# Fourier mixing and RWKV channel mix: half of batch 1's first x load moved ahead of the receptance weights

## The chip, the cores and the metric

The kernel runs on one core of a Trainium2 chip. The metric is device time in microseconds (us); lower is better. A profiled execution lists every instruction of the engines: TensorE (PE in the profile, its weight loads PEld), VectorE (DVE), ScalarE (ACT), GpSimd (POOL) and SyncE (SP), and the traffic of the 16 DMA engines.

## The reference

The input x has 8 batches of 3072 rows and 256 columns, in fp32. First comes a Fourier mixing, then an RWKV channel mix on its result:

```python
X = np.fft.fft(np.fft.fft(x, axis=1), axis=2).real
x_prev = X shifted by one row, first row zero
xk = mu_k * X + (1 - mu_k) * x_prev
xr = mu_r * X + (1 - mu_r) * x_prev
k = np.maximum(xk @ w_k, 0)                 # 256 -> 1024
out = sigmoid(xr @ w_r) * ((k * k) @ w_v)   # w_r 256 -> 256, w_v 1024 -> 256
```

## The kernel before, in words

**The work per batch.** The sequence of 3072 rows is cut into 96 groups of 32 rows (batch 0), or into two sets of 48 (batches 1 to 7; one set on partitions 0 to 47, the other on partitions 64 to 111). Each batch is loaded in two halves, h = 0 and 1. A half consists of a direct part, `xp` (9 or 8 rows of 256 for each partition, `load_p`, L129), and of a mirrored part, `xm` (`load_m`, L144, an indirect gather of 8 rows for each partition, and for h = 0 one more row, `load_m0`). Both are cast from fp32 to fp16 on the way. `fold` (L161) adds `xp` to `xm` read backwards into `p`, on VectorE; its two instructions are L173 and L175. `butterfly` (L206) or `quarters_1` and `quarters_2` split `p` further. Then follow the sequence transform in two matmul stages with a twist between them (`a_...`, `d_...`, `c_...`; evacuated from PSUM by L572 on VectorE or L574 on ScalarE), the token shift with mu (`diff` L856, `scaled` L868, `mixed` L879), and the channel mix in chunks of 512 rows: `k_products` (L914), relu (L924), square (L934 on VectorE or L932 on ScalarE), the receptance in `r_item` (L941, sigmoid L946), the value in `v_tile` (L955) or, for the first chunks, in four parts in `v_part` (L967), and the final product `v_out` (L977 on VectorE, then an output DMA from SyncE).

**Buffers.** `xp` and `xm` have three buffers each, taken in turn by half batch (`x_tiles`, L120). Half (1, 0) uses xp buffer 1, half (1, 1) buffer 2, half (2, 0) buffer 0, half (2, 1) buffer 1, half (3, 0) buffer 2. PSUM gives three tiles psW of two banks and two tiles psV of one bank.

**The padding rows.** A few matmuls read partitions 0 to 111 of the folded data as a whole, with zero weights on partitions 48 to 63. What lies there must be a number. In batches 1 to 3 `load_p` therefore reads 64 partitions for the first set rather than 48. From batch 4 on it reads 48, and what is left in the buffers from before serves as padding.

**The order of the work.** The order is written out by hand. A loop over steps (L1245) emits for each step a piece of a chunk's key product and then what is listed for this step: `at(step, f, ...)` and `event(step, ...)`, L1107 to L1239. `pin_order` (L89) then keeps each engine in the order in which the instructions were emitted. An engine that waits holds everything behind it.

**The queue of loads.** All casting loads and gathers are issued by POOL, in order. `load_gate` (L495) lets VectorE write a single element that POOL then overwrites (L497), so that POOL cannot run ahead of VectorE past this point. At the time in question POOL issues: `loads` (L479: the key weights `wk` for forward chunks, the value weights `wv_sb`, some index tables), then `loads_0` (a gate, then the two receptance gathers `wr_sb[0]`), at step 1 `loads_1` (a gate, then half (1, 0): the two sets of `xp`, the single mirrored row, the large mirrored gather), at step 4 `loads_2` (two key gathers, half (1, 1), two receptance gathers, the identity table of `quarter_rows`), and at steps 9, 12 and 13 the halves (2, 0), (2, 1) and (3, 0). The receptance weights are read first by `r_item` at step 5. The fold of half (1, 0) stands at step 8, that of half (1, 1) at step 11, that of half (2, 0) at step 16.

Of the kernel before, what the change touches and what calls it, by code (L numbers as in the profile page):

```python
# [39 lines left out]
def kernel(  # L40
# [10 lines left out]
    nc = tc.nc  # L51
# [4 lines left out]
    N1, R = 48, 64  # L56
# [52 lines left out]
    xp_sb = [const.tile([112, 9, 256], FP16, name=f"xp{n}") for n in range(3)]  # L109
# [10 lines left out]
    def x_tiles(b, h):  # L120
        xp_t[b, h] = xp_sb[(2 * b + h - 1) % 3] if b or h else xp_00
        xm_t[b, h] = xm_sb[(2 * b + h) % 3]
# [3 lines left out]
    def parts(b):  # L126
        return 112 if b else 96

    def load_p(b, h, q0=0):  # L129
        r, n = 9 * h + q0, 9 - h - q0  # L130
        if b:
            for g in range(2):
                k = 64 if g == 0 and b < 4 else N1
                src = dataclasses.replace(x[b, 32 * g + r:32 * g + r + 1, :],
                                          ap=[[64 * D, k], [D, n], [1, D]])
                nc.gpsimd.dma_start(out=xp_t[b, h][64 * g:64 * g + k, 0:n], in_=src)  # L136
            return
        src = dataclasses.replace(x[b, r:r + 1, :], ap=[[32 * D, 96], [D, n], [1, D]])
        nc.gpsimd.dma_start(out=xp_t[b, h][0:96, q0:q0 + n], in_=src)

    def gather(dst, src, idx):
        nc.gpsimd.indirect_dma_start(dst, None, src, bass.IndirectOffsetOnAxis(ap=idx, axis=0))  # L142

    def load_m(b, h, o, n, idx):  # L144
        gather(xm_t[b, h][0:parts(b), XM0 + o:XM0 + o + 256 * n],
               x.rearrange("b (s r) d -> (b s) (r d)", r=n), idx)

    def load_m0(b):
        if b == 0:
            gather(xm_00[:, 1:257], x.rearrange("b s d -> (b s) d"), idx_0[:, 0:1])  # L150
        else:
            load_m(b, 0, 2048, 1, idx_g0[:, b:b + 1])

    def load_xh(b, h):
        x_tiles(b, h)
        load_p(b, h)
        if h == 0:
            load_m0(b)
        load_m(b, h, 0, 8, idx_g8[:, b, h:h + 1])
# [102 lines left out]
    for h in range(2):  # L262
        x_tiles(0, h)
    load_p(0, 0, 5)
    for xm in xm_sb:
        V.memset(_v(xm, XM0 + 2048, [(256, 2)]), 0.0)
# [22 lines left out]
    iota(idx_4, pattern=[[-1, 2]], base=S // 4 - 3, channel_multiplier=-8)  # L289
    load_m(0, 0, 0, 8, idx_8[:, 0, 0:1])  # L290
    load_p(0, 1)
    load_m(0, 1, 1024, 4, idx_4[:, 0:1])
    load_m(0, 1, 0, 4, idx_4[:, 1:2])
# [163 lines left out]
    turn = const.tile([P, P], FP16)  # L457
    mu_n = const.tile([P, 2, 2], FP32)

    def mirrored_mu():  # L460

        for a in range(2):
            V.tensor_copy(out=mu_m[:, a], in_=mu_f[:, 1 - a])
        V.tensor_copy(out=mu_m[0:1], in_=mu_f[0:1])
# [30 lines left out]
    def load_gate():  # L495
        V.memset(gate, 0)  # L496
        iota(gate, pattern=[[0, 1]], base=0, channel_multiplier=0)  # L497

    def loads_0():
        load_gate()  # L500
        for a in range(2):
            gather(wr_sb[0][a], moe_w_r, row_i[:, a:a + 1])

    def loads_1():
        load_gate()
        load_xh(1, 0)

    def loads_2():
        for a in range(2):
            gather(wk_sb[1][a], moe_w_k, row_i[:, 2 + a:3 + a])  # L510
        load_xh(1, 1)
        for a in range(2):
            gather(wr_sb[1][a], moe_w_r, row_i[:, 2 + a:3 + a])
        quarter_rows()

    def eo_sine():
# [27 lines left out]
    def quarter_rows():  # L544
        iota(same_i, pattern=[[0, 2], [1, 64]], base=0, channel_multiplier=-1)
        nc.gpsimd.tensor_scalar(out=same, in0=same_i, scalar1=0.0, scalar2=None,
                                op0=ALU.is_equal)
# [562 lines left out]
    diff(0, 4, 8)  # L1110
    mix_part(0, 0, 4, 8)
    loads_0()
    d_small(0, 10, 2)
    diff(0, 8, 16)
# [4 lines left out]
    event(3, (half_tables,))  # L1119
    event(4, (c_item, 0, 17, 8))  # L1120
    at(1, loads_1)
    at(4, loads_2)
    at(8, fold, 1, 0)
    at(5, r_item, (0, 0, 0))
    at(5, c_item, 0, 25, 2)
    at(5, diff, 0, 16, 24)
    at(5, mirrored_mu)
    at(6, mix_part, 0, 0, 16, 24)
    at(9, butterfly, 1, 0, 1)
# [3 lines left out]
    at(9, r_item, (0, 0, 1))  # L1133
    at(9, mix, 0, 0, 1, 1)
    at(9, load_xh, 2, 0)
    at(10, mix_part, 0, 1, 16, 24)
    event(11, (a_sums, 1, 0, 0), (a_sums, 1, 0, 4))
# [164 lines left out]
```

## Time and profile before

| what | value |
|---|---|
| median of 3 runs | 427.22 us (426.31 to 427.66) |
| profiled execution | 426.86 us |
| its span, from the first to the last instruction | 425.1 us |
| granted TensorE clock | 0.998 |
| VectorE busy | 371.7 us (87%) |
| ScalarE busy | 332.4 us (78%) |
| GpSimd busy | 63.2 us (15%) |

How to read it: a row of the timeline has the start of the instruction or of a group of equal ones, the busy time, the engine, the line of the code, the operation, what is written and read, and the number of instructions. Brackets at its end give the engine's idle time just before it and what ended that. Matmuls are pipelined, and their ends are modelled, so two groups can overlap in the list; the starts are what to compare. In the answer by stretches each engine has its busy time and in parentheses its instructions; then come the granted clock, the mean busy share of the 16 DMA engines (it can go a little over 1, since packets overlap) and GB/s.

### The profile page before, as it was taken

The numbers are of one execution on the slowest core, as the hardware profiler recorded it, in microseconds if no ns is written. First come the engines' busy times: TensorE is split into PE (matmuls) and PEld (weight loads), VectorE is DVE, ScalarE is ACT, GpSimd is POOL, SyncE is SP. The second block draws the span as 40 slices with busy tenths as digits, with TensorE's granted clock in tenths as the row PEclk, the third lists the DMA queues.
The fourth block names the chain that finished last, engine by engine and source line by source line (L and its number), as shares of the span: only waits on it lengthen the run. The fifth ranks groups of instructions, "written<-read, shape, count | busy, mean of one in ns | idle before, by whom it ended". The sixth has DMA issues, their size and how long they took to land.

```text
span 425.1 us, 9716 instructions
## 1 busy us (share of the span) xinstructions
PE 417.9 (98%) x4008; PEld 292.8 (69%) x4008; DVE 371.7 (87%) x593; ACT 332.4 (78%) x438; POOL 63.2 (15%) x99
## 2 busy tenths in 40 slices
PE   8999999999999999999999999999999999999996
PEld 3766766776767767676767776777777776776765
DVE  8998999999898999989999899989999676977553
ACT  7889887698769986699767996689876897666661
POOL 7478400200060001400032000500000000000000
PEclk9999999999999999999999999999999999999999
DMA  8879972632376222942349232772233232332333
GB/s 171 111 115 212 229 162 56 123 92 69 74 141 157 57 70 56 210 107 51 71 75 227 51 76 55 136 173 59 52 74 76 53 75 51 74 74 53 74 76 99
DMA packets 35280, 42.64 MB, mean 100 GB/s; under 512 B 4146, under 2 KB 31140, under 8 KB 35236
## 3 DMA queue, kind: packets, MB, share of 16 engines
q1 hardware_dynamic: 27488, 25.41, 24.0%
q0 software_dynamic: 7440, 16.36, 22.2%
q8 instruction: 31, 0.51, 0.5%
q10 hardware_dynamic: 308, 0.26, 0.2%
q14 instruction: 13, 0.11, 0.1%
HBM read 33.20 MB, written 25.17 MB: 137 GB/s over the span
## 4 chain that ended last, share of the span: by engine, by line
PE 90%; DVE 6%; DMA 2%; issue 1%; POOL 1%; ACT 0%; DVEq 0%; POOLq 0%
PE psV L955 37%; PE psW L914 36%; PE psW L941 9%; PE psW L591 3%; DMA xm<-in_x_dram,idx_g 2%; PE psV L967 1%; DVE p L173 1%; PE psV L591 1%; DVE rl L309 1%; PE psW L699 1%; PE psW L677 1%; DVE x L879 1%; DVE t L868 1%; DVE g_all L572 0%; DVE k L934 0%
## 5 line engine op out<-in xcount | busy, mean ns | idle before, releaser
L924 ACT ACTIVATE rl<-psW 128x1024 f16<-128x1024 f32 x192 | 194.4, 1039 | 79.1 <-PE psW L914 75.5
L914 PE MATMUL psW<-x,wk 128*128 128x512 f16 (+1 forms) x776 | 194.4, 377 | 0.3 <-DVE x L1051 0.3
L955 PE MATMUL psV<-wv_sb,k 128*128 128x256 f16 x1424 | 184.2, 273 | 0.0
L955 PEld LDWEIGHTS <-k 128*128 128x128 f16 x1424 | 136.7, 98 | 38.9
L934 DVE TENSOR_TENSOR k<-rl 128x2048 f16<-128x2048 f16 (+1 forms) x100 | 115.6, 1157 | 32.8 <-ACT rl L924 32.6
L914 PEld LDWEIGHTS <-wk 128*128 128x128 f16 x776 | 75.5, 98 | 53.8 <-issue 0.4
L977 DVE SCALAR_TENSOR_TENSOR o<-psV,r 128x512 f32<-128x512 f32 (+1 forms) x97 | 65.8, 681 | 9.8 <-PE psV L955 8.9
L879 DVE TENSOR_TENSOR x<-y,t 128x1536 f16<-128x1536 f16 (+3 forms) x76 | 62.4, 827 | 2.2
L946 ACT ACTIVATE r<-psW 128x1024 f16<-128x1024 f32 x48 | 50.0, 1041 | 0.8 <-PE psW L941 0.8
L941 PE MATMUL psW<-wr,x 128*128 128x256 f16 x384 | 49.8, 273 | 0.0
L941 PEld LDWEIGHTS <-x 128*128 128x128 f16 x384 | 37.5, 98 | 13.9
L574 ACT ACTIVATE a<-psW 128x832 f16<-128x832 f32 (+4 forms) x36 | 28.7, 851 | 1.0 <-PE psW L658 0.6
L142 POOL DMA_INDIRECT xm<-in_x_dram,idx_g x21 | 26.2, 1249 | 6.8 <-issue 6.1
L574 ACT ACTIVATE g_all<-psW 128x512 f16<-128x512 f32 (+5 forms) x47 | 26.6, 646 | 0.3 <-PE psW L699 0.2
L497 POOL IOTA gate<- 1x1 int32 x7 | 0.8, 121 | 163.5 <-DVE gate L496 163.5
L173 DVE TENSOR_TENSOR p<-xp,xm 112x2304 f16<-112x2304 f16 (+4 forms) x19 | 21.7, 1141 | 1.1 <-DMA xm<-in_x_dram,idx_g 1.1
L868 DVE TENSOR_SCALAR t<-d,muf_t 128x1536 f16<-128x1536 f16 (+3 forms) x44 | 22.1, 513 | 0.1
L574 ACT ACTIVATE pq<-psW 128x1024 f16<-128x1024 f32 (+1 forms) x21 | 20.4, 1007 | 0.1
L868 DVE TENSOR_SCALAR t<-d,mu_m 128x1536 f16<-128x1536 f16 x32 | 19.6, 613 | 0.0
L856 DVE TENSOR_TENSOR d<-y 128x1664 f16<-128x1664 f16 (+5 forms) x19 | 16.7, 880 | 0.4 <-ACT y L574 0.4
L848 DVE TENSOR_TENSOR y<-pq 128x960 f16<-128x960 f16 (+3 forms) x28 | 15.7, 603 | 0.4
L136 POOL DMA_DIRECT2D xp<-in_x_dram x28 | 15.7, 572 | 1.7 <-DMA xm<-in_x_dram,idx_g 0.8
(155 smaller groups left out, 229.0 us busy)
## 6 DMA issues: line engine op xcount, KB each, us to landing
out_dram<-o SPq DMA_DIRECT2D x189, 128.0 KB, 2.4
xp<-in_x_dram POOLq DMA_DIRECT2D x11, 216.0 KB, 5.2
xp<-in_x_dram POOLq DMA_DIRECT2D x12, 192.0 KB, 7.0
xp<-in_x_dram POOLq DMA_DIRECT2D x3, 288.0 KB, 9.5
xp<-in_x_dram POOLq DMA_DIRECT2D x3, 256.0 KB, 9.9
wv_sb<-in_moe_w_v_dram POOLq DMA_DIRECT2D x1, 512.0 KB, 8.4
xp<-in_x_dram SPq DMA_DIRECT2D x1, 480.0 KB, 4.3
xp<-in_x_dram POOLq DMA_DIRECT2D x1, 384.0 KB, 6.1
```

Source lines behind the costliest of these rows:

```text
L142: nc.gpsimd.indirect_dma_start(dst, None, src, bass.IndirectOffsetOnAxis(ap=idx, axis=0))
L173: V.tensor_tensor(out=p[:, q0:q0 + n], in0=xp[:, q0:q0 + n], in1=_v(xm, o + 256, [(-256, n), (-1, 256)]), op=ALU.add)
L574: nc.scalar.activation(out=out_ap, in_=in_ap, func=AF.Copy)
L868: V.tensor_scalar(out=dst, in0=src, scalar1=mu, scalar2=None, op0=ALU.mult)
L879: V.tensor_tensor(out=_v(x_t[b, j, m], o, [(64 * step, hi - lo), (step, 64)]), in0=y_t[b][:, lo + 3 * m:hi + 3 * m, a], in1=x_t["t", a][:, ...
L914: nc.tensor.matmul(out=st["k", ds][:, 512 * hs + lo:512 * hs + hi], lhsT=wk_sb[m][a][:, 128 * fc:128 * fc + 128], rhs=xk[:, a, 512 * i + l ...
L924: nc.scalar.activation(out=st["rl"][:, 2 * ds:2 * ds + 2], in_=st["k", ds].rearrange("p (f t) -> p f t", f=2), func=AF.Relu, bias=0.0, sca ...
L934: V.tensor_tensor(out=k2_t[c][:, lo:hi], in0=r, in1=r, op=ALU.mult)
L941: nc.tensor.matmul(out=ps[:, 256 * tb:256 * tb + 256], lhsT=x_t[b, 1, m][:, a, 512 * i + 128 * tb: 512 * i + 128 * tb + 128], rhs=wr_sb[m] ...
L946: nc.scalar.activation(out=st["r", c], in_=ps, func=AF.Sigmoid)
L955: nc.tensor.matmul(out=st["v", tb - h][:, 256 * h:256 * h + 256], lhsT=k2_t[c][:, fc, 128 * tb:128 * tb + 128], rhs=wv_sb[:, fc], start=(f ...
L977: V.scalar_tensor_tensor(out=o.rearrange("p a b -> p (a b)")[:, 0:256 * n], in0=st["v", t0][:, 0:256 * n], scalar=16.0, in1=st["r", c][:, ...
```

## The change

- The load of the first set of half (1, 0), that is 64 partitions of 9 rows, moves from `loads_1` to `loads_0`, behind the same gate as the two receptance gathers and ahead of them. The second set (48 partitions), the single row and the large gather stay in `loads_1`.
- Batches 2 and 3 read 48 partitions for the first set, as batches 4 to 7 do. Only batch 1 still reads 64.
- The padding of one row, row 8, in xp buffers 0 and 2 is no longer written by a load of 64 partitions before it is read. Two memsets on POOL (`zero_rows`) write partitions 32 to 63 of that row, in `loads_2` behind the second receptance gathers.

```diff
-    def load_p(b, h, q0=0):
+    def load_p(b, h, q0=0, gs=(0, 1)):
         r, n = 9 * h + q0, 9 - h - q0
         if b:
-            for g in range(2):
-                k = 64 if g == 0 and b < 4 else N1
+            for g in gs:
+                k = 64 if (b, g) == (1, 0) else N1
...
-    def load_xh(b, h):
-        x_tiles(b, h)
-        load_p(b, h)
+    def load_xh(b, h, gs=(0, 1)):
+        if 0 in gs:
+            x_tiles(b, h)
+        load_p(b, h, 0, gs)
...
+    def zero_rows():
+        for n in (0, 2):
+            nc.gpsimd.memset(xp_sb[n][32:64, 8], 0.0)
+
...
     def loads_0():
         load_gate()
+        x_tiles(1, 0)
+        load_p(1, 0, 0, (0,))
         for a in range(2):
             gather(wr_sb[0][a], moe_w_r, row_i[:, a:a + 1])
 
     def loads_1():
         load_gate()
-        load_xh(1, 0)
+        load_xh(1, 0, (1,))
 
     def loads_2():
...
         load_xh(1, 1)
         for a in range(2):
             gather(wr_sb[1][a], moe_w_r, row_i[:, 2 + a:3 + a])
+        zero_rows()
         quarter_rows()
```

## The prediction, made before the result was known

> **What bounds the kernel now.** I read the page's summary first, then TensorE (PE) in order of time, then VectorE (DVE), the chain that ended last, the DMA load by stretches, and GpSimd (POOL).
>
> ```profile
> span 425.1 us, 9716 instructions
> PE 417.9 (98%) x4008; PEld 292.8 (69%) x4008; DVE 371.7 (87%) x593; ACT 332.4 (78%) x438; POOL 63.2 (15%) x99
> ```
>
> The profiled execution took 426.86 us, 1.76 us more than its span, and 0.36 us less than the median 427.22. PE is busy 98% of the span, so there is little to win: only time in which PE stands still counts. Two answers by stretches say where that can be (columns: stretch and, for each engine, busy us; then granted clock, DMA share, GB/s; the second answer is one stretch, 62 to 416 us).
>
> ```profile
> 19.00:22.00 3.00, 3.00 (x27) 1.98 (x26) 2.96 (x11) 2.56 (x4) 1.67 (x3) 1.00 0.06 7
> 22.00:24.00 2.00, 2.00 (x21) 1.51 (x20) 2.00 (x7) 2.00 (x3) 1.37 (x4) 1.00 0.53 65
> 24.00:26.00 2.00, 2.00 (x28) 1.33 (x25) 2.00 (x6) 1.30 (x3) 1.70 (x2) 1.00 0.74 78
> 26.00:34.00 8.00, 8.00 (x64) 5.31 (x59) 6.58 (x18) 7.04 (x8) 6.47 (x8) 1.00 0.98 160
> 34.00:58.00 24.00, 23.48 (x261) 16.47 (x259) 23.23 (x38) 20.86 (x25) 11.81 (x14) 1.00 1.09 228
> ```
> ```profile
> 62.00:416.00 354.00, 354.00 (x3386) 249.82 (x3384) 310.82 (x427) 278.22 (x354) 28.06 (x38) 1.00 0.39 88
> ```
>
> From 62 us on PE has no idle time at all: whatever it is early or late by at 62 us, it is at the end. In 34 to 58 us it lacks half a microsecond, DVE is busy 23.23 of 24, and the DMA engines are full (1.09). In 19 to 22 us the DMA engines stand idle (0.06). PE in order of time (start, us, work):
>
> ```profile
> 38.57 1.03 PE L914 MATMUL psW<-x,wk 128*128 128x512 f16 x4
> 39.67 1.20 PE L967 MATMUL psV<-wv_sb,k 128*128 128x256 f16 x8
> 40.80 0.91 PE L658 MATMUL psW<-w_hh,p 48*128 48x104 f16 x32
> ```
> ```profile
> 49.26 1.06 PE L699 MATMUL psW<-w_eo,a 128*128 128x128 f16 x16
> 50.65 0.60 PE L967 MATMUL psV<-wv_sb,k 128*128 128x256 f16 x4 [0.33 <-DVE o L977]
> 51.08 1.03 PE L914 MATMUL psW<-x,wk 128*128 128x512 f16 x4
> 51.95 0.61 PE L699 MATMUL psW<-w_eo,a 128*128 128x128 f16 x8
> 52.39 1.04 PE L967 MATMUL psV<-wv_sb,k 128*128 128x256 f16 x8
> 53.27 1.03 PE L914 MATMUL psW<-x,wk 128*128 128x512 f16 x4
> 54.13 0.28 PE L699 MATMUL psW<-w_eo,a 128*128 128x128 f16 x2
> 54.24 1.04 PE L941 MATMUL psW<-wr,x 128*128 128x256 f16 x8
> 55.39 0.18 PE L754 MATMUL psW<-g_all,turn 128*128 128x13 f16 x1
> ```
>
> Read the starts, since the ends are modelled. Undisturbed, four matmuls of 512 columns take 0.87 us (51.08 to 51.95), eight of 256 take 0.88 (52.39 to 53.27), eight of 128 take 0.44 (51.95 to 52.39). Against that PE loses 1.10 - 0.87 = 0.23 ahead of 39.67 and 1.13 - 0.88 = 0.25 inside that group (gap A, 0.48); 1.39 - 2 x 0.44 = 0.51 ahead of 50.65 (gap B); 1.15 - 0.88 = 0.27 ahead of 55.39 (gap C). Together 1.26 us. DVE beside them:
>
> ```profile
> 34.04 1.36 DVE L173 TENSOR_TENSOR p<-xp,xm 112x2304 f16<-112x2304 f16 x1 [0.56 <-DMA xm<-in_x_dram,idx_g]
> ...
> 42.50 1.23 DVE L173 TENSOR_TENSOR p<-xp,xm 112x2048 f16<-112x2048 f16 x1 [0.49 <-DMA xm<-in_x_dram,idx_g]
> ```
>
> These are its two folds of batch 1, each with its idle time ahead of it. Its evictions that PE waits for:
>
> ```profile
> 38.93 1.28 DVE L977 SCALAR_TENSOR_TENSOR o<-psV,r 128x512 f32<-128x512 f32 x2
> ...
> 49.91 1.28 DVE L977 SCALAR_TENSOR_TENSOR o<-psV,r 128x512 f32<-128x512 f32 x2
> ```
> ```profile
> 53.44 1.35 DVE L173 TENSOR_TENSOR p<-xp,xm 112x2304 f16<-112x2304 f16 x1
> 54.83 0.20 DVE L175 TENSOR_TENSOR p<-xp,xm 112x9 f16<-112x9 f16 x1
> 54.92 0.42 DVE L572 CAST g_all<-psW 128x256 f16<-128x256 f32 x1
> ```
>
> Each gap ends as a DVE instruction ends. The two evictions from 38.93 end at about 39.57 and 40.21, and PE needs their two psV banks at 39.67 and halfway through; the first from 49.91 ends at about 50.55, PE goes on at 50.65; the cast from 54.92 ends at 55.34, PE goes on at 55.39. DVE itself is late because the two folds wait for their mirrored x: 0.56 us at 34.04 and 0.49 at 42.50. So up to 1.05 us of PE time hangs on two gathers. The first of them, in the chain that ended last:
>
> ```profile
> 26.58 7.33 DMA xm<-in_x_dram,idx_g
> ```
>
> It is issued at 26.58 and lands at 33.91, while the DMA engines are full (0.98 in 26 to 34 us). It stands behind the xp loads of the same half batch.
>
> **The change part by part.** POOL's queue around the moved load:
>
> ```profile
> 20.15 1.15 POOL L142 DMA_INDIRECT wr<-in_moe_w_r_dram,row_i  x1 [0.17 <-issue]
> 21.59 0.96 POOL L142 DMA_INDIRECT wr<-in_moe_w_r_dram,row_i  x1 [0.30 <-issue]
> 23.08 0.12 POOL L497 IOTA gate<- 1x1 int32 x1 [0.52 <-DVE gate L496]
> 23.31 1.23 POOL L136 DMA_DIRECT2D xp<-in_x_dram  x2
> 24.84 1.44 POOL L142 DMA_INDIRECT xm<-in_x_dram,idx_g  x1 [0.30 <-issue]
> 26.58 1.13 POOL L142 DMA_INDIRECT xm<-in_x_dram,idx_g  x1 [0.30 <-issue]
> ```
>
> *Issue.* One of the two xp issues at 23.31 (1.23 / 2 = 0.61 us) goes to 20.15. The receptance gathers start 0.61 + 0.30 = 0.91 later, at 21.06 and 22.50, and end at 23.46. The second gate, which waited for DVE until 23.08, now comes at about 23.46. From there 0.23 + 0.61 + 0.30 + 1.44 + 0.30 = 2.88 us lead to the large mirrored gather: 26.34, 0.24 earlier than now. Alone that is too little.
>
> *Transfer.* The moved load writes 64 x 9 x 256 x 2 bytes = 295 KB. Now it moves behind the receptance weights, just ahead of the full stretch; after the change it begins about 21.5 us, in the idle one. (The weights' bytes appear from 22 us, 0.7 us after their first issue ends at 21.30; the moved load's issue ends at 20.76.) Everything behind it in a full DMA stretch comes earlier by what it would have taken there: 1.8 us at 160 GB/s (26 to 34 us), 1.3 at 228, 3.8 at 78, and only 0.24 if issue sets the pace. I take 1.8, from the stretch in which the first gather moves. The first gather then lands at 33.91 - 1.8 = 32.1, and DVE is ready for it at 34.04 - 0.56 = 33.48. The second lands near 42.4 now; DVE will be ready at 42.50 - 0.49 - 0.56 = 41.45, so it needs a lead of 1.05 us and has 1.8. Both waits go, and DVE gains 1.05 us.
>
> A rule of the Trainium skill bears on the rate: the page "SBUF — State Buffer", section "Door 1: The DMA port swizzle", says that a transfer to partitions 0 to 63 reaches only half of the DMA ports, measured at 196 GB/s. An estimate by it: 1.5 us, and the same sum. No row here shows this load by itself; 24 to 26 us, where it moves with its neighbour, has 78 GB/s, less than the rule gives.
>
> *What PE gets.* Gap A: both evictions could start 0.56 earlier and end at 39.0 and 39.65, ahead of PE's own 39.44 and 39.44 + 0.44; their inputs come from the matmuls ahead of 38.57. Gap A goes whole, PE gains 0.48. Gap B: DVE releases at 50.55 - 1.05 = 49.50; PE arrives at 50.14 - 0.48 = 49.66; B goes too, PE is 0.99 ahead. Gap C: DVE ends the cast at 55.34 - 1.05 = 54.29, PE arrives at 55.12 - 0.99 = 54.13; about 0.16 to 0.2 of C stays, and PE's lead ends at DVE's 1.05. What is late next is this cast, behind the fold from 53.44. I take 1.0 us, a little under the cap, since ScalarE (20.86 of 24 us busy) must follow at each step.
>
> *Receptance weights.* They are moved behind the load, and PE reads them here:
>
> ```profile
> 26.94 1.04 PE L941 MATMUL psW<-wr,x 128*128 128x256 f16 x8
> ```
> ```profile
> wr<-in_moe_w_r_dram,row_i POOLq DMA_INDIRECT x1, 2.7
> ```
>
> That row is the gather of 21.59: it lands at 24.3. Issued at 22.50 it lands at 25.2, 1.7 us ahead of the matmuls, if the transfer ahead does not hold it. Zero, with that cover.
>
> *Fewer rows in batches 2 and 3.* Sixteen partitions less, for 9, 8, 9 and 8 rows of 512 bytes: 74, 66, 74 and 66 KB. Three of the four fall into the full stretch: 213 KB, 0.9 us of DMA time at 228 GB/s, all of it after the two gathers above in POOL's order. The next reader, the fold at 53.44, waits for nothing now. Zero.
>
> *Two memsets* of 32 x 256 on POOL go behind the last weight gathers and ahead of:
>
> ```profile
> 34.29 1.96 POOL L142 DMA_INDIRECT wr<-in_moe_w_r_dram,row_i  x1 [0.30 <-issue]
> 36.27 0.27 POOL L545 IOTA same_i<- 128x128 int32 x1
> ```
>
> Each costs POOL between 0.12 (the gate's one element) and 0.90 us at the far end, half of the slowest row here; I take 0.27, by the nearest kind. That puts off the identity table and batch 2's loads by 0.5 us, less than the 0.9 us of transfer that the cut rows give back, and DVE does not wait for batch 2. They write a row that batch 1's loads leave alone, so they need wait for none of them. Zero.
>
> Sum: 426.86 - 1.0 = 425.86 for the profiled execution; 427.22 - 1.0 = **426.2 us** for the median.
>
> **The rivals.**
>
> *The second gather does not move.* If the pace behind the first gather is set by POOL's issues, its lead shrinks to 0.24 and DVE waits again at 42.50. Then DVE's later instructions stand where they stood, PE is halted at 50.65 as now, and the 0.48 won at gap A is lost again there: 427.2, or up to 426.7 with half a lead. For it: POOL issues without a pause from 23 us. Against it: a DMA share of 0.98 and then 1.09. Chance 0.2. That the change does nothing ends at the same time.
>
> *All three gaps close.* If the cast of gap C is passed by as well, PE gets its 1.26 us: 426.0, and 425.7 if the slack between groups goes with it. For it: C would be only 0.2 wide. Against it: DVE has no other idle time than 1.05 us before it. Chance 0.15.
>
> *The receptance weights come late*, the case on the other side. Their matmuls at 26.94 would halt PE, and everything behind moves with them. At 78 GB/s the moved load lasts from 21.5 to 25.3, the weights behind it another 2.0 us (131 KB at the 65 GB/s of 22 to 24 us): 27.3, a stall of 0.35. If POOL's issues stretch too, as the gather at 34.29 (1.96 instead of 0.96 us) while DVE folds, the load starts 1 us later and each gather follows by as much: 28.3 or later, a stall of 1.4, and 426.2 + 1.4 = 427.6. It costs more than the change brings from a landing at 28.0 on, and over 0.3% from 29.3 on. Chance 0.08.
>
> The Trainium skill has a rule for that stretching, on the page "SBUF — State Buffer", section "SBUF: two separate sides": DVE and GpSimd share a port pair under an exclusive lock, and DMA descriptors written by GpSimd wait while DVE holds it. This trace agrees in direction: 1.96 us beside the fold. But the gathers at 20.15 and 21.59 ran beside a DVE busy 2.96 of 3 us and took 1.15 and 0.96.
>
> **How the numbers follow.** The forecast (both waits gone, 0.8 to 1.2 us won) has 0.57. What a measurement of this kernel can tell from no change is about 0.3%, 1.28 us; the three runs of before span 1.35 us. The forecast lies just short of that line, so a quarter of it counts as faster, with most of the three-gaps case: 0.27 in all. Slower by over 0.3% takes the late weights at their worst: 0.05. The rest, 0.68, is within 0.3%. The range goes from 425.4, the three-gaps case with some spread below it, to 427.3, the second gather unmoved; it leaves out the late weights' bad end and the tails.
>
> **What would show it.** Right: no wait for xm ahead of the folds of batch 1; the DMA share in 21 to 24 us near full; the L967 groups of 39.67 and 50.65 starting 0.2 to 1 us earlier and without a gap; L941's first group still near 26.9. Wrong: a wait at L941 for wr; a wait that stays at the second fold; POOL's memsets waiting for a load; or a PE start at 62 us no earlier although the folds are.

## The result, and the profile after

| | median | lowest to highest | runs |
|---|---|---|---|
| before | 427.27 us | 426.31 to 429.07 | 22 |
| changed | 426.19 us | 425.83 to 428.12 | 22 |

The ratio is 0.9979, with a 95% interval of 0.997 to 0.9988: the change saves 0.2%, some 0.9 us. The ratio, here and below, is estimated from all executions and is not the quotient of the two medians. The forecast was 426.2 us. The page after the change:

```profile
span 424.2 us, 9718 instructions
PE 417.3 (98%) x4008; PEld 292.8 (69%) x4008; DVE 371.7 (88%) x593; ACT 332.5 (78%) x438; POOL 64.8 (15%) x101
```

The span is 0.9 us shorter. PE after the change, in order of time. In this and the next views L922 is what L914 was, L975 was L967, L666 was L658, L707 was L699, L762 was L754, L949 was L941, and on VectorE L174 was L173, L580 was L572, L876 was L868, L985 was L977.

```profile
38.56 1.03 PE L922 MATMUL psW<-x,wk 128*128 128x512 f16 x4
39.42 1.04 PE L975 MATMUL psV<-wv_sb,k 128*128 128x256 f16 x8
40.39 0.91 PE L666 MATMUL psW<-w_hh,p 48*128 48x104 f16 x32
...
48.85 1.06 PE L707 MATMUL psW<-w_eo,a 128*128 128x128 f16 x16
49.81 0.60 PE L975 MATMUL psV<-wv_sb,k 128*128 128x256 f16 x4
...
53.40 1.04 PE L949 MATMUL psW<-wr,x 128*128 128x256 f16 x8
54.55 0.18 PE L762 MATMUL psW<-g_all,turn 128*128 128x13 f16 x1
...
62.53 1.04 PE L949 MATMUL psW<-wr,x 128*128 128x256 f16 x8
```

PE stands where it stood at 38.56 (38.57 before). It is 0.41 us ahead at 40.39, 0.84 at 49.81 and at 54.55, and 0.84 at the last row, which started at 63.37. Gap A lost 0.40 of its 0.48, gap B 0.43 of 0.51, gap C nothing: from 53.40 to 54.55 it is 1.15 us as before. DVE beside it:

```profile
33.18 1.36 DVE L174 TENSOR_TENSOR p<-xp,xm 112x2304 f16<-112x2304 f16 x1
...
38.39 1.29 DVE L985 SCALAR_TENSOR_TENSOR o<-psV,r 128x512 f32<-128x512 f32 x2 [0.33 <-PE psV L975]
...
41.48 1.25 DVE L174 TENSOR_TENSOR p<-xp,xm 112x2048 f16<-112x2048 f16 x1
...
45.26 0.67 DVE L876 TENSOR_SCALAR t<-d,mu_m 128x1536 f16<-128x1536 f16 x1
...
47.45 0.72 DVE L876 TENSOR_SCALAR t<-d,mu_m 128x1536 f16<-128x1536 f16 x1
...
54.08 0.42 DVE L580 CAST g_all<-psW 128x256 f16<-128x256 f32 x1
```

Neither fold waits. DVE is 0.86 us ahead at the first fold, 0.54 at 38.39 where it now waits for PE, 1.02 at the second fold, and 0.84 at the cast. The queue of POOL, the DMA share, and the first gather's landing:

```profile
20.08 0.63 POOL L136 DMA_DIRECT2D xp<-in_x_dram  x1
21.01 1.29 POOL L142 DMA_INDIRECT wr<-in_moe_w_r_dram,row_i  x1 [0.30 <-issue]
22.60 1.22 POOL L142 DMA_INDIRECT wr<-in_moe_w_r_dram,row_i  x1 [0.30 <-issue]
23.84 0.14 POOL L502 IOTA gate<- 1x1 int32 x1
23.92 0.59 POOL L136 DMA_DIRECT2D xp<-in_x_dram  x1
24.81 1.50 POOL L142 DMA_INDIRECT xm<-in_x_dram,idx_g  x1 [0.30 <-issue]
26.62 1.14 POOL L142 DMA_INDIRECT xm<-in_x_dram,idx_g  x1 [0.30 <-issue]
```
```profile
22.00:24.00 2.00, 2.00 (x21) 1.48 (x20) 2.00 (x7) 2.00 (x3) 1.69 (x4) 1.00 0.69 123
24.00:26.00 2.00, 2.00 (x28) 1.33 (x25) 2.00 (x6) 1.29 (x3) 1.70 (x2) 1.00 0.91 89
26.00:34.00 8.00, 8.00 (x65) 5.34 (x60) 7.23 (x19) 7.05 (x8) 6.48 (x8) 1.00 0.89 146
```
```profile
xm<-in_x_dram,idx_g POOLq DMA_INDIRECT x1, 5.3
```

The large gather is issued at 26.62, no earlier than before (26.58), since the two receptance gathers now take 1.29 and 1.22 us. It lands at 31.9 instead of 33.9. The DMA share in 26 to 34 us is no longer full (0.89 instead of 0.98).

**One DMA engine decides the landing.** The packets of this gather in the two traces show where the 2 us come from. It has 112 packets of 4096 bytes, seven for each of the 16 DMA engines; one that is not held up takes about 0.32 us. The first starts at 28.41 us before and at 28.45 after, both times 0.7 us after POOL has ended the issue (27.71 and 27.76). The 100th ends at 31.75 before and at 31.35 after: 0.4 us. The last ends at 33.57 before and at 31.62 after: 1.95 us. Before, one packet starts at 30.12, when the other engines have long begun (28.41 to 29.38), and takes 1.44 us; just six follow it one by one, 0.31 us apart. The trace does not name the engine of a packet, but seven in a row are one engine's share, and in e1, f2 and f4 below all 112 sort into 16 rows of seven. So I read them as one engine that began late and began with a long packet. From 29.29 to 30.12 the trace has no packet of another transfer, so bytes queued ahead did not hold that engine then. After, no packet that starts over 1.4 us behind the first takes more than 0.44. So nearly all of the gather was on time in both, and a single engine's share was late in one.

### The profile page after: what moved, and what is told of

Read it like the earlier page. It is cut to its first block, busy times and chain, and to the rows that moved or that the text cites. A ratio compares the mean times of both kernels' runs of the same rounds, so it can differ in the third digit from the quotient of the medians.

```text
span 424.2 us, 9718 instructions
## 1 busy us (share of the span) xinstructions
PE 417.3 (98%) x4008; PEld 292.8 (69%) x4008; DVE 371.7 (88%) x593; ACT 332.5 (78%) x438; POOL 64.8 (15%) x101
## 4 chain that ended last, share of the span: by engine, by line
PE 95%; DVE 3%; issue 0%; POOL 0%; ACT 0%; POOLq 0%; DVEq 0%
PE psW L922 39%; PE psV L963 37%; PE psW L949 10%; PE psW L599 3%; PE psV L975 3%; PE psV L599 1%; DVE rl L310 1%; DVE p L174 1%; PE psW L685 1%; PE psW L707 1%; DVE g_all L580 0%; DVE o L985 0%; PE psW L651 0%; DVE k L942 0%; DVE rw L310 0%
## 5 line engine op out<-in xcount | busy, mean ns | idle before, releaser
L922 PE MATMUL psW<-x,wk 128*128 128x512 f16 (+1 forms) x776 | 194.4, 377 | 0.3 <-DVE x L1059 0.3
L922 PEld LDWEIGHTS <-wk 128*128 128x128 f16 x776 | 75.5, 98 | 53.8 <-issue 0.4
L985 DVE SCALAR_TENSOR_TENSOR o<-psV,r 128x512 f32<-128x512 f32 (+1 forms) x97 | 65.8, 681 | 10.0 <-PE psV L963 8.9
L949 PE MATMUL psW<-wr,x 128*128 128x256 f16 x384 | 49.8, 273 | 0.0
L949 PEld LDWEIGHTS <-x 128*128 128x128 f16 x384 | 37.5, 98 | 13.9
L876 DVE TENSOR_SCALAR t<-d,muf_t 128x1536 f16<-128x1536 f16 (+3 forms) x44 | 22.0, 512 | 0.1
L174 DVE TENSOR_TENSOR p<-xp,xm 112x2304 f16<-112x2304 f16 (+4 forms) x19 | 21.7, 1142 | 0.0
L876 DVE TENSOR_SCALAR t<-d,mu_m 128x1536 f16<-128x1536 f16 x32 | 19.8, 618 | 0.0
```

Of the source, the lines that this page charges most:

```text
L174: V.tensor_tensor(out=p[:, q0:q0 + n], in0=xp[:, q0:q0 + n], in1=_v(xm, o + 256, [(-256, n), (-1, 256)]), op=ALU.add)
L876: V.tensor_scalar(out=dst, in0=src, scalar1=mu, scalar2=None, op0=ALU.mult)
L922: nc.tensor.matmul(out=st["k", ds][:, 512 * hs + lo:512 * hs + hi], lhsT=wk_sb[m][a][:, 128 * fc:128 * fc + 128], rhs=xk[:, a, 512 * i + l ...
L949: nc.tensor.matmul(out=ps[:, 256 * tb:256 * tb + 256], lhsT=x_t[b, 1, m][:, a, 512 * i + 128 * tb: 512 * i + 128 * tb + 128], rhs=wr_sb[m] ...
L985: V.scalar_tensor_tensor(out=o.rearrange("p a b -> p (a b)")[:, 0:256 * n], in0=st["v", t0][:, 0:256 * n], scalar=16.0, in1=st["r", c][:, ...
```

## The experiments

My theory after the result: DVE's two waits for the gathers are what PE lost, and the moved transfer takes them away. The rivals: the cut rows do part of it; the first wait alone counts; the receptance weights are close to being late. Later, when the profiles disagreed, a second theory came up: the late engine is a matter of chance, and what counts is how much cover the gather has.

All profiles at a glance. S is the start of the first key products, R the start of the receptance group that stood at 63.37 us before. "Long packet" is the longest one of the first gather that starts over 1.4 us after its first. In all fourteen the span is R plus 361.6 to 361.8 us, so R tells the time, and nothing after 62 us matters.

| profile | S | R | R - S | long packet | waits of the folds |
|---|---|---|---|---|---|
| before | 18.15 | 63.37 | 45.22 | 1.44 | 0.56, 0.49 |
| changed | 18.14 | 62.53 | 44.39 | 0.44 | none |
| e1 move only | 18.75 | 64.26 | 45.51 | 1.51 | 0.62, 0.70 |
| e2 cut only | 18.52 | 63.78 | 45.26 | 1.94 | 1.18 |
| e3 load again | 18.14 | 62.36 | 44.22 | 0.50 | none |
| e4 second only | 19.37 | 65.72 | 46.35 | 1.01 | 0.78, 0.16 |
| e5 fold behind cast | 18.14 | 64.87 | 46.73 | 1.85 | 1.57 |
| e6 weights late | 18.15 | 64.28 | 46.13 | 0.33 | none |
| e8 quiet POOL | 18.14 | 62.33 | 44.19 | 0.34 | none |
| e9 both | 18.14 | 65.19 | 47.05 | 1.75 | 1.10, 0.83 |
| f1 change again | 19.00 | 63.60 | 44.60 | 0.36 | none |
| f2 move only again | 18.68 | 64.55 | 45.87 | 1.76 | 1.26, 0.21 |
| f3 gates early | 18.15 | 63.63 | 45.48 | 0.45 | none |
| f4 gates early, no move | 18.73 | 63.22 | 44.49 | 0.72 | none |

A packet of over 1 us comes with a wait of the folds in all seven profiles that have one, and no profile without it shows a wait. In all seven just six packets follow the long one.

**e1: the move alone.** All 64 rows are read in batches 2 and 3, and there are no memsets.

```diff
-                k = 64 if (b, g) == (1, 0) else N1
+                k = 64 if g == 0 and b < 4 else N1
...
-        zero_rows()
```

> The load is moved, but batches 2 and 3 still read 64 partitions and the two memsets are left out. Theory (the gain is the moved transfer, which takes both DMA waits off VectorE's folds): no wait for xm at either fold of batch 1, the receptance group that starts at 63.37 us before starts at 62.5, and the time is 426.2 us, as with the whole change. Rival (the cut rows relieve the full DMA stretch and make part of the gain): the lead at 62.5 is halved or less, and the time is 426.7 or more.

Measured: 427.0 us against 427.33, ratio 0.9999 (0.9984 to 1.0015). The theory's forecast failed. Its profile shows why for that execution: the long packet is there (its engine began at 30.92 us, the others by 29.58), and both folds wait.

**e2: the cut alone.**

```diff
     def loads_0():
         load_gate()
-        x_tiles(1, 0)
-        load_p(1, 0, 0, (0,))
...
-        load_xh(1, 0, (1,))
+        load_xh(1, 0)
```

> The rows of batches 2 and 3 are cut and the memsets are in, but the load stays where it was. Theory: both waits stay, 0.56 us and 0.49 us, the receptance group starts at 63.4 as before, and the time is 427.2 us. Rival (the cut rows make part of the gain): the second wait is shorter and the time is 426.8 or less.

Measured: 427.2 us, ratio 0.9998 (0.9986 to 1.001). No gain of the cut rows by themselves is seen. Its profile has no second wait, since DVE is already 1.18 us late from the first. The bulk of the first gather is as early as with the move: counted from S, its 100th packet ends at 13.34 us here, at 13.60 in the profile of before, and at 13.20 to 13.42 in eight profiles with the move (changed, e1, e3, e5, e8, e9, f1, f2). So even the 0.4 us of the bulk is not clearly the move's.

**e3: the transfer put back behind the gather.**

```diff
+    spare = const.tile([96, 6, 256], FP16)
+
+    def again():
+        src = dataclasses.replace(x[1, 0:1, :], ap=[[32 * D, 96], [D, 6], [1, D]])
+        nc.gpsimd.dma_start(out=spare, in_=src)
+
     def loads_2():
+        again()
```

> The whole change, and behind the first mirrored gather a spare load of the same 295 KB (96 partitions of 6 rows into a tile that nothing reads). The first fold keeps its lead, the second gather loses it again. Theory (what is won at the first fold is given back where VectorE next waits): no wait at the first fold, a wait of about half a microsecond at the second, the value group of 39.67 us still near 39.4, and a receptance group back at 63.3 or so: 427.1 us. Rival (the gain is won at the first gap and stays won): the group at 62.95 and 426.7 us.

Neither came. In the profile no fold waits and R is 62.36, the best but one. The 100th packet of the second gather ends at 40.64 instead of 39.67 us, 1.0 later, as 295 KB more should do, and its last at 40.97 instead of 40.58, before DVE is ready at 41.50. So with the change the second gather's last packet has 0.9 us of cover (40.58 against 41.48), and the spare load takes only 0.4 of it. The landing itself comes some 0.3 us after the last packet (31.62 and 31.9 at the first gather), so the cover is nearer 0.6. Ten executions spread from 425.78 to 428.96 us (median 426.73, ratio 1.0008, 0.9991 to 1.0026); with less cover the bad ones seem to come more often, but ten are too few to show that.

**e4: only the second gather relieved.**

```diff
-            for g in range(2):
+            for g in range(1 if (b, h) == (1, 1) else 2):
...
         iota(idx_g0[0:1], pattern=[[S, B]], base=0, channel_multiplier=0)
+        nc.gpsimd.memset(xp_sb[2][64:112, 0:8], 0.0)
```

> The kernel before, without the second set's direct load of half (1, 1): a memset early on POOL puts zeros on these partitions instead, so that part of batch 1's transform is left out. 197 KB less stand ahead of the second gather; the first is untouched. Theory: the first fold still waits 0.56 us, the second no longer; PE's gap ahead of 39.67 stays, that ahead of 50.65 shrinks by about 0.45, the receptance group starts at 62.9, and the time is 426.7 us. Rival (only the first wait counts): the group stays at 63.4, 427.2 us.

Measured: 428.55 us, ratio 1.0042 (1.0025 to 1.0059). It does not answer its question, since the memset on POOL cost more than the gap. POOL and DVE in its profile:

```profile
15.29 1.80 POOL L491 MEMSET xp<- 48x2048 f16 x1
```
```profile
15.72 1.42 DVE L1033 COPY g<-g_all 128x127 f16<-128x127 f16 x1
```

A copy of 127 elements, 0.19 us elsewhere, ends at 17.14, just after POOL's memset. S is 1.2 us late from there on. The granted clock fell as well, to 0.53 in 19.3 to 21 us and 0.54 in 21 to 23, and the eight key matmuls begun at 19.37 took 1.86 us; so R - S is 1.13 longer than before, and R measures neither wait.

**e5: the fold of batch 2 behind the cast of gap C.**

```diff
-    at(16, fold, 2, 0)
+    at(17, fold, 2, 0)
```

> The whole change, and the first fold of batch 2 one step later, behind the cast of L580 that ended PE's third gap (0.27 us ahead of 55.39 before, ahead of 54.55 after). Theory (the third gap stayed since VectorE's lead and PE's are then the same 0.84 us, and the fold of 1.35 us stands ahead of the cast): the gap goes, PE starts its group of 13 columns 0.2 us earlier, the receptance group at 62.53 moves to 62.3, and the time is 425.9 to 426.0 us. Rival (the gap is TensorE's own, a change of tile shape): nothing moves, 426.2 us.

Measured: 428.18 us against 427.03, ratio 1.0025 (1.0008 to 1.0041). The profile shows both halves of the answer, the gap in its first two rows and what came instead in the third:

```profile
54.64 1.04 PE L949 MATMUL psW<-wr,x 128*128 128x256 f16 x8
55.52 0.19 PE L762 MATMUL psW<-g_all,turn 128*128 128x13 f16 x1
...
60.55 1.02 PE L922 MATMUL psW<-x,wk 128*128 128x512 f16 x4 [1.13 <-DVE pq L580]
```

Gap C is closed: 0.88 from start to start instead of 1.15. So it was DVE's, as forecast; f1 below, where the gap closes without this edit, agrees. But the fold now stands ahead of the cast of `pq`, and PE waits 1.13 us for that. What is won at one place is paid four times over at the next. R came 2.34 us later than with the change because this execution has the long packet too; the fastest of the 12, 426.99 us, lies 1.16 above the change's fastest (425.83), which is about the 1.13.

**e6: the receptance weights behind the whole half batch.**

```diff
     def loads_0():
         load_gate()
-        x_tiles(1, 0)
-        load_p(1, 0, 0, (0,))
+        load_xh(1, 0)
...
     def loads_1():
         load_gate()
-        load_xh(1, 0, (1,))
```

> The whole half (1, 0), with its second set and both mirrored gathers, stands ahead of the receptance weights. About 1 MB more is ahead of them, at 160 GB/s some 4.5 us more than with the change. Theory (the weights are a deadline at 26.93 us with about 1 us of cover in the change): PE waits at the first receptance group, which starts at 28 to 30 us, and the receptance group of 62.53 starts later by that less what the folds gain: 427 to 429 us. Rival (the weights still slip through, or the stall is absorbed): 26.9 and 426.2 us.

```profile
28.83 1.10 PE L947 MATMUL psW<-wr,x 128*128 128x256 f16 x8 [1.72 <-DMA wr<-in_moe_w_r_dram,row_i]
```

Measured: 428.1 us, ratio 1.0031 (1.0017 to 1.0045). PE comes to this group 1.9 us late, and R is 1.75 later than with the change. This run's theory held, and the price of late weights is as the prediction's rival had it, nearly one for one. With the change itself the weights are on time: the group starts at 26.93 us.

**e8 and e9: a quiet POOL, and both edits together.**

```diff
-    at(12, load_xh, 2, 1)
...
-    at(13, load_xh, 3, 0)
+    at(18, load_gate)
+    at(18, load_xh, 2, 1)
+    at(18, load_xh, 3, 0)
```

> The whole change, and the loads of halves (2, 1) and (3, 0) put off to step 18 behind a gate, so that POOL issues nothing between about 43 and 57 us. Theory (VectorE lost 0.18 us of its lead of 1.02 between 41.5 and 49.1 us because two multiplications ran beside POOL's issues, 0.67 and 0.72 us instead of 0.61): they take 0.61, VectorE's eviction of 49.07 comes at 48.9, PE's receptance group at 62.3 to 62.4, the time 426.0 us. Rival (the difference is chance, or comes from the DMA traffic): 49.07 and 426.2 us.

Measured: 426.13 us against 427.03, ratio 0.9992 (0.9978 to 1.0006). R is 62.33 as the theory had it, but the reason it gave is not shown. e3, where POOL issues in this stretch as usual, has the short multiplications too:

```profile
45.26 0.61 DVE L883 TENSOR_SCALAR t<-d,mu_m 128x1536 f16<-128x1536 f16 x1
...
47.38 0.61 DVE L883 TENSOR_SCALAR t<-d,mu_m 128x1536 f16<-128x1536 f16 x1
```

So that POOL issues in this stretch is not enough to lengthen them: it does so in before, e1, e3, e4, e5 and f2, and both are short there (0.61 or 0.62). One of the two is longer (0.67 to 0.71) in e2, e6, f1, f3 and f4, which have the issues too, and both are short in e8 and e9, which have none. Whether an issue at a certain moment lengthens them stays open; the 0.18 us that DVE lost (0.67 and 0.72 instead of 0.61) came in the changed kernel's first profile and not in all.

> The two edits before together (the fold behind the cast, and a quiet POOL). Theory: the gains add where both bind, receptance group at 62.1 to 62.2, 425.8 us. Rival: no better than the better one of them.

Measured: 427.49 us, ratio 1.0013 (0.9998 to 1.0029). It has e5's wait of 1.13 us and the long packet besides.

**f1 and f2: the change and the move alone, on one chip.** Their code is that of the change and of e1.

> The whole change as it is, beside the next run on the same chip. The traces so far show that the landing of the first mirrored gather differs from execution to execution by over 2 us (31.9 us in the changed kernel's profile, 34.3 in one with the same instructions up to there), so the change should shift how often VectorE waits, and not take the waits away for good. Theory: median 0.5 to 1 us below the kernel before, the fastest executions of both near 425.8. Rival (the waits go for good, and what differs is the start of the kernel): all executions below the kernel before by the same 0.8 us.

> The move without the cut rows and the memsets, once more, beside the whole change on one chip. Up to 36 us both issue the same loads. Theory (the cut rows come after the gathers and change nothing): the same median as the whole change within 0.4 us, and the same two groups of times. Rival (the cut rows count): slower than the whole change by 0.7 us, as the two earlier medians on different chips were (427.0 and 426.2).

Measured: f1 426.9 us, f2 427.95 us, the kernel before 427.67 on this chip. The ratios are 0.9986 (0.997 to 1.0002) and 1.0002 (0.9987 to 1.0018). The fastest executions lie together (426.21, 426.39, before 426.21), as f1's theory had it, though it put them near 425.8: the kernel before can be as fast. That it is so less often fits the medians, but f1's interval just includes no change. f1's profile has no wait of the folds, and gap C is closed, 0.89 us from start to start, while PE loses time elsewhere:

```profile
54.73 1.04 PE L949 MATMUL psW<-wr,x 128*128 128x256 f16 x8
55.62 0.18 PE L762 MATMUL psW<-g_all,turn 128*128 128x13 f16 x1
```
```profile
43.22 1.62 ACT L582 ACTIVATE a<-psW 128x832 f16<-128x832 f32 x2 [1.42 <-PE psW L922]
```

PE has 0.29 us too much ahead of 44.14 and 0.25 ahead of 47.64, behind ScalarE, which begins this eviction late. Such a late eviction, with no cause that the trace shows, stands in all four profiles taken on this chip (f1 to f4) and in none of the other ten, so the medians of the f runs may hold it too. The kernel before was at best 426.21 us on this chip, and 425.75 beside e8.

But f2's theory failed a second time: the move alone shows no gain. Its first fold in the profile:

```profile
35.07 1.36 DVE L174 TENSOR_TENSOR p<-xp,xm 112x2304 f16<-112x2304 f16 x1 [1.26 <-issue]
```

That is DVE idle for 1.26 us ahead of the fold; the profile puts no name to it, and the long packet of 1.76 us is in the same place as in the others, ahead of the last six.

**f3 and f4: both gates earlier, with and without the change.** The edit is the same in both:

```diff
+    loads_0()
     diff(0, 4, 8)
     mix_part(0, 0, 4, 8)
-    loads_0()
...
-    at(1, loads_1)
+    at(0, loads_1)
```

> The whole change with both gates earlier: the first group of loads is emitted ahead of VectorE's first difference (gate at about 18.5 instead of 19.85 us), the second at step 0 instead of step 1. The DMA engines are idle from 19.2 us on, so the moved load begins about 1.3 us earlier, and POOL's whole queue with it: the first mirrored gather is issued near 25.3 instead of 26.6 and lands 1.3 us earlier. Theory: no wait at either fold in nearly every execution, median 425.9 to 426.0, and 425.8 for the fastest. Rival (the loads collide with the value weights, which land at 20 to 21 us and are read at 22.4, or the landing time is set by something else): a wait of PE at 22.4, or no difference from the whole change.

> The kernel before with both gates earlier by the same edit, and the load where it was. Theory: the large mirrored gather is issued at 25.3 instead of 26.6 us and lands 1.3 us earlier, less than the move brings by its transfer (2.0 us) but enough for both waits in the profile of before (they needed 0.56 and 1.05): 426.2 to 426.4 us. Rival (only the moved transfer counts): 427.2 us.

Measured: f4 426.29 us, all 12 executions between 426.10 and 427.19, ratio 0.9977 (0.9964 to 0.9989): the gain of the change, without it. Its first gather is issued at 25.38 instead of 26.58 us although that execution started 0.58 later, and the 100th packet ends at 30.54, about 1.8 us earlier against the start. f3 has the change as well, and gained nothing: 427.61 us, ratio 1.0004 (0.999 to 1.0017), no execution below 427.03. No fold waits in its profile. The time is lost elsewhere:

```profile
27.89 1.02 ACT L582 ACTIVATE y<-psW 128x1024 f16<-128x1024 f32 x1 [2.11 <-PE psW L922]
```

ScalarE begins this eviction 1.7 us later than in the changed kernel (26.17), while the matmuls it reads began at 25.53 in f3 and 25.50 in the change. PE loses 1.04 us behind it. The releaser named is not what it reads, and the trace shows no cause for this stall; it is of the kind that f1 and f2 have. f4 has the best median of this chip, and its ratio (0.9977) is level with the change's (0.9979): neither is shown to beat the other.

## Why the prediction was right, and where it was not

**What bounds the kernel: right.** The span follows R in all fourteen profiles, and in before, changed, e1, e2, e3 and e8 R follows the two folds and the three gaps. In the others something else adds to it: the late weights (e6), the wait for `pq` (e5, e9), a lower clock (e4), late evictions on ScalarE (f1 to f4).

**Issue: near.** The large gather was to be issued at 26.34; it was at 26.62. The two receptance gathers took 0.4 us more than before.

**Transfer, the step that failed.** "I take 1.8" for the lead of everything behind the moved load. The landing came 2.0 us earlier, which looks right, but the packets show that the bulk gained 0.4 at most, near the low end that the prediction named (0.24): POOL's issue set its pace, since the issue came no earlier and the first packet started 0.7 us after it in both. The other 1.6 us are one engine's late start and long first packet, present in the profile of before and absent after. It is also there in four profiles with the moved load (e1, f2, e5 and e9). So the move does not take the waits away, it makes them rarer at best. That the landing came out near the forecast was luck, and the time of 426.2 us was met in part for a reason that the prediction did not have.

**What PE gets: right in kind and nearly in size.** Forecast 1.05 at most and 1.0 taken; the profile has 0.84, and e3 and e8, without the two long multiplications, 1.01 and 1.04. Gap A keeps 0.09 us in the change and again in e3, e8, f1 and f4, where no fold waits; this part was presumably never DVE's. Gap B keeps 0.08 in the change but only 0.01 in e3, e8 and f1, so the 0.08 was DVE's, behind the two longer multiplications. Gap C was said to keep 0.16 to 0.2 of 0.27 and kept all of it in this profile; it kept 0.15 in e3 and 0.08 in e8, and nothing in f1. DVE met the new wait for PE at 38.39 (0.33 us), where the prediction let it go on unhindered; gap A closed all the same.

**Receptance weights: right.** They were on time, and e6 measured what lateness costs (R 1.75 us later for 1.9 of lateness).

**Rows and memsets: not settled.** The cut alone shows no gain (e2), as forecast. But the whole change gained in its 22 runs, and in the 12 of f1 by 0.14% with an interval that just includes nothing, while the move without the cut showed no gain in 24 executions on two chips (e1, f2). Against the change beside it on one chip, the move alone was 1.05 us slower in the median, but their intervals overlap. Up to 36 us both issue the same loads at the same distances (the large gather 6.77 us after the first gate in the change's profile, in e1's and in f2's), and the waits come before that. I know of no way from the cut rows to the long packet. With the move and the cut two of six profiles have one (e5, e9, but not changed, e3, e8, f1), with the move alone both: too few to tell. Whether there is a way, or chance made the difference, stays open. What makes an engine late stays open too.

**The rivals.** The second gather had cover to spare (e3). The late weights did not come. That all three gaps close did not come in the profile above; in f1's, of the same kernel, they do but for 0.1 us, and PE loses 0.54 elsewhere. e5 shows what it costs to force the third.

## What to carry to other kernels

A load lands when the last of its 16 engines is done: look at when the last packets end and when the bulk does, and give a load enough cover for one engine's bad luck (2 us here), which an earlier gate gave as well as the changed order (f4). Before putting a gain down to bytes moved ahead, see whether the queue behind them is held by issue; here it was (the gather was issued at 26.58 us before and at 26.62 after). A wait of half a microsecond that one profile shows may be there in one execution and not in the next, so compare several profiles before explaining it.

## What the runs showed of the hardware

- In a gather of 112 packets of 4096 bytes, one packet that starts 1.4 us or more after the first can take 1.0 to 1.9 us instead of 0.32, and the six behind it, 0.31 us apart, are late by that and by its late start. This came in seven of the fourteen first gathers (in six at over 1.4 us). In the profile of before the packet started 1.70 us after the first of the gather, in e1 1.86, in f2 1.99, in e4 2.55.
- A memset of 48 x 2048 on POOL took 1.80 us, and a DVE copy begun under it ended with it, after 1.42 us instead of 0.19 (e4). The Trainium skill, page "SBUF — State Buffer", section "SBUF: two separate sides", says that DVE and GpSimd lock their shared port pair for a whole instruction; this pair of rows agrees with it.
- Beside a fold on DVE, a gather's issue on POOL took 2.37 us in the changed kernel:

```profile
33.02 2.37 POOL L142 DMA_INDIRECT wr<-in_moe_w_r_dram,row_i  x1 [0.30 <-issue]
```

The fold ran from 33.18 to 34.54. Before, the gather beside the fold took 1.96 us. That the fold caused it is not shown.
